# An H3 convolution and ReLU MLP kernel on one core: wider stores and sums of convolution units, row statistics on ScalarE, a new table of moves

## The chip, the cores and the metric

The kernel runs on one core of a Trainium2 chip. The metric is the device time of one execution in microseconds (us). The shown runs of the kernel before took 848.18, 848.7 and 849.46 us; their median is 848.7 us. Below, PE is TensorE, DVE is VectorE, ACT is ScalarE, POOL is GpSimd and SP is SyncE, which issues most of the transfers.

## What is computed

A sequence of 2048 rows of 640 features goes through four layers. Layers 1 and 3 are a gated long convolution, layers 2 and 4 a two-matrix MLP with ReLU. All inputs are float32.

```python
def A(q, k, v, shift_k, ssm_k, ssm_D):        # q is layernorm(x)
    k_shift = sum over t of k shifted by 3 - t, times shift_k[:, 3 - t]
    kv = k_shift * v
    y = irfft(rfft(kv, 2 * S) * rfft(ssm_k, 2 * S))[:S]   # causal, per feature
    return q * (y + kv * ssm_D)
def B(x, w1, w2):                             # x is layernorm(x)
    return maximum(x @ w1, 0) @ w2            # 640 -> 1728 -> 640
x = x + A(layernorm(x), ...); x = x + B(layernorm(x), ...)
x = x + A(layernorm(x), ...); x = x + B(layernorm(x), ...)
```

The convolution's result depends on k, v and the filters alone, so it is computed once and read by both convolution layers.

## The kernel before

**Convolution.** The sequence is cut into 8 chunks of 256 rows, the features into 5 tiles of 128. A unit is one tile of a chunk or two of them: two tiles of one chunk, or one tile of two neighbouring chunks. `transform` makes the spectra of a unit: `at` of kv, `gt` of the filter, 768 numbers per partition and tile (real part, imaginary part, their sum). `spills` (L787 to L791) stores them to DRAM tensors `A` and `G`, one per chunk and tile. `products` multiplies and sums: output chunk a takes the sum over c of A of chunk c times G of chunk a - c. Each product is a DVE `tensor_mul` into a tile `pd` (L847), or straight into the accumulator `pacc` for the first one (L844), and each further one is added by a DVE `tensor_add` of 768 numbers (L848). The spectra of earlier chunks are loaded again at L835. Then come three DVE operations (L878, L880, L881) and one transform back on PE; the result `ys` goes to a DRAM tensor `Y` at L931, one store of 128 x 128 for each tile and each half (row stripe) of a chunk. Tile `ys` lives in a ring `u` of two buffers, which the results `u` of L878 and L880 use too, so a store that has not yet read `ys` holds such a buffer.

**Rows and MLP.** A stripe is 128 rows of a chunk. For the first two chunks each stripe is a step of its own, later both stripes of a chunk go together. `prep` loads `y` from `Y` (L1162), makes the layernorm statistics in `stats`, gates (L1165), adds to the residual `x` (L1172), makes statistics again and cuts the normalized rows into two float16 parts that a transposing DMA brings into `xT` (L1230). In `stats`, DVE forms the negative mean `negm` from the row sums (L1097), ACT the squares (L1100), the root, a Newton step (L1108 to L1112) and the scaled rows (L1122). `main` runs the MLP in seven blocks of hidden features: `mm1` makes `h` in PSUM (L1361 to L1376), ACT writes its high part `hh` (L1516), DVE its low part (L1517; for a single stripe both parts lie in one tile, so this row also reads `hh<-h,hh`), and `mm2` multiplies by w2 one block later (L1345 to L1348). For the last two chunks a form with seven instead of eight block products is used (L1296, L1406). At the end DVE adds to `x` (L1588) with a sum over the row in `sp`; L1596 adds the two parts of that sum into `sums`, which `stats` of the next layer reads.

**Order.** The program records every operation in `Plan` and lays them out with a planner: `order` is a list scheduler that takes, on every engine, the ready operation with the smallest key; `latest` computes from its result the latest time at which each operation may start, and these times are the next keys. `MOVES` is a table: an empty entry means one round of `latest`, another entry (seed, size, from, to, share) shifts the keys of a random share of the operations with a key in that stretch. After the table is worked through, the last order is issued. So an engine executes its instructions in a fixed order, and one that waits holds back all that stands behind it on its engine.

Names in the listings: `hh2_1` is the hidden block 1 of MLP step 2 (steps 0 to 3 are chunk 0: stripe 0 and 1 of the first MLP, stripe 0 and 1 of the second; steps 4 to 7 chunk 1); `pacc2_0`, `pd2_0_4`, `u02_0` belong to the unit that starts at chunk 2, tile 0; `x0_1` is stripe 1 of chunk 0, and `xnA0_1_11`, `negmB0_1_1` belong to its second layer pair (layer 1, stripe 1).

Of the kernel before, what the change touches and what calls it, by code (L numbers as in the profile page):

```python
# [428 lines left out]
def tile_h3_mlp(ctx: ExitStack, tc: tile.TileContext, q, kT, vT, shk, hF, hR, dD, w1, w2, cM, cG, out):  # L429
# [371 lines left out]
    def products(u, at, gt, after):  # L801
# [18 lines left out]
        else:  # L820
            for i, (a, t) in enumerate(u):
                macs += [(i, c, a - c, t) for c in range(a + 1)]
# [926 lines left out]
```

## Time and profile before

| | us |
|---|---|
| median of the shown runs | 848.7 |
| the profiled execution's own time | 848.15 |
| its span in the profile | 846.4 |
| outside the span | 1.75 |

The profile gives for each engine the time in which it was busy. A matmul's record runs until its result has landed, so records overlap, and a short gap between two matmuls does not show as idle time. A row of a group ends with the idle time just before its instructions and what ended it. The mean granted TensorE clock is 0.999 of full speed. Lines with an L are lines of the kernel before; after the change the same statements stand 62 to 88 lines further down (L1517 is then L1605, L848 is L925, L1097 is L1185, L1596 is L1684).

### The profile page before, as it was taken

What the parts mean: (1) busy time and instruction counts of PE and PEld (TensorE: products, weight loads), DVE (VectorE), ACT (ScalarE), POOL (GpSimd) and SP (SyncE); (2) the same over time, 40 slices, a digit from 0 to 9 for tenths busy, and PEclk for the clock granted to TensorE, in tenths of its full rate; (3) what the DMA queues carried; (4) which work ended last, traced back from release to release, by engine and by line L of the source; (5) the groups of instructions that cost most, each with busy time, mean ns of one, the idle gap of its engine ahead of it and who ended that gap; (6) DMA issues with size and microseconds to landing.
All of it is one profiled execution on the core that took longest, in us unless ns stands there. A gap on an engine that the chain in (4) does not pass through costs nothing.

```text
span 846.4 us, 20221 instructions
## 1 busy us (share of the span) xinstructions
PE 835.7 (99%) x7937; PEld 667.4 (79%) x7937; DVE 786.7 (93%) x1514; ACT 510.4 (60%) x1182; POOL 43.8 (5%) x54
## 2 busy tenths in 40 slices
PE   8999999999999999999999999999999999999998
PEld 6987877878878768777787777777777788888886
DVE  7999989999999999999999999999998789989675
ACT  4898587446777565746457474565524487767531
POOL 0000000000001010000100000000000000000000
PEclk9999999999999999999999999999999999999999
DMA  9995868985999999988996977778898466060300
GB/s 312 391 329 193 249 187 233 284 300 167 297 299 248 313 238 279 242 207 234 230 309 180 248 210 207 193 183 220 250 285 271 135 202 142 16 169 13 57 33 33
DMA packets 144914, 181.70 MB, mean 215 GB/s; under 512 B 55089, under 2 KB 98865, under 8 KB 144818
## 3 DMA queue, kind: packets, MB, share of 16 engines
q1 hardware_dynamic: 136498, 169.92, 66.1%
q0 software_dynamic: 8320, 10.49, 7.8%
q8 instruction: 62, 1.02, 0.5%
q14 instruction: 34, 0.28, 0.1%
HBM read 124.59 MB, written 34.08 MB: 187 GB/s over the span
## 4 chain that ended last, share of the span: by engine, by line
PE 76%; DVE 12%; ACT 4%; DMA 3%; issue 2%; SPq 1%; DVEq 0%; ACTq 0%
PE h L1373 8%; PE h L1374 8%; PE h L1376 8%; PE o L1296 7%; PE o L1345 7%; PE o L1346 7%; PE o L1348 6%; PE h L1361 3%; DVE pd L847 2%; DVE pacc L848 2%; PE oc L1345 2%; PE oc L1346 2%; PE oc L1348 2%; PE h L1363 2%; PE h L1406 1%
## 5 line engine op out<-in xcount | busy, mean ns | idle before, releaser
L1373 PE MATMUL h<-xT,w 128*128 128x256 f16 (+1 forms) x1030 | 237.4, 250 | 0.5 <-DVE hh L1531 0.2
L1374 PE MATMUL h<-xT,w 128*128 128x256 f16 (+1 forms) x1030 | 237.3, 250 | 0.0
L1376 PE MATMUL h<-xT,w 128*128 128x256 f16 (+1 forms) x1030 | 237.3, 250 | 0.0
L848 DVE TENSOR_TENSOR pacc<-pacc,pd 128x768 f32<-128x768 f32 x140 | 133.9, 957 | 0.6
L1345 PE MATMUL o<-w,hh 128*128 128x512 f16 x336 | 127.4, 379 | 0.0
L1346 PE MATMUL o<-w,hh 128*128 128x512 f16 x336 | 127.4, 379 | 0.0
L1374 PEld LDWEIGHTS <-w 128*128 128x128 f16 x1130 | 110.6, 98 | 15.8 <-issue 1.5
L1373 PEld LDWEIGHTS <-w 128*128 128x128 f16 x1130 | 110.5, 98 | 14.8
L1376 PEld LDWEIGHTS <-w 128*128 128x128 f16 x1030 | 100.8, 98 | 6.6
L1516 ACT ACTIVATE hh<-h 128x512 f16<-128x512 f32 (+1 forms) x97 | 46.7, 481 | 90.8 <-PE h L1376 64.6
L1345 PEld LDWEIGHTS <-hh 128*128 128x128 f16 x672 | 65.7, 98 | 28.3 <-issue 0.6
L1346 PEld LDWEIGHTS <-hh 128*128 128x128 f16 x672 | 65.8, 98 | 27.1
L847 DVE TENSOR_TENSOR pd<-Ax,Gx 128x768 f32<-128x768 f32 x83 | 78.9, 956 | 2.3 <-DMA Gx<-G 2.3
L1348 PE MATMUL o<-w,hl 128*128 128x512 f16 x208 | 78.9, 379 | 0.0
L1345 PE MATMUL oc<-w,hh 128*128 128x128 f16 x336 | 73.8, 220 | 0.0
L1346 PE MATMUL oc<-w,hh 128*128 128x128 f16 x336 | 73.7, 219 | 0.0
L1348 PEld LDWEIGHTS <-hl 128*128 128x128 f16 x416 | 40.7, 98 | 24.9 <-DVE hl L1517 0.4
L1361 PE MATMUL h<-xT,w 128*128 128x256 f16 (+1 forms) x400 | 57.3, 251 | 0.4 <-DMA xT<-xh 0.4
L589 ACT ACTIVATE tp<-kt,shs 128x256 f32<-128x256 f32 (+1 forms) x78 | 44.4, 576 | 21.2 <-DVE acc L663 14.7
L1348 PE MATMUL oc<-w,hl 128*128 128x128 f16 x208 | 45.6, 219 | 0.2 <-DVE hl L1517 0.2
L847 DVE TENSOR_TENSOR pd<-at,Gx 128x768 f32<-128x768 f32 x46 | 43.5, 957 | 0.0
L1361 PEld LDWEIGHTS <-w 128*128 128x128 f16 x400 | 36.0, 98 | 5.2 <-issue 0.7
(272 smaller groups left out, 1978.7 us busy)
## 6 DMA issues: line engine op xcount, KB each, us to landing
Ax<-A SPq DMA_DIRECT2D x89, 384.0 KB, 4.4
Gx<-G SPq DMA_DIRECT2D x89, 384.0 KB, 4.4
G<-gt SPq DMA_DIRECT2D x30, 384.0 KB, 4.3
A<-at SPq DMA_DIRECT2D x30, 384.0 KB, 6.1
ws<-in_w SPq DMA_DIRECT2D x28, 320.0 KB, 6.5
y<-Y SPq DMA_DIRECT2D x22, 320.0 KB, 3.4
x<-in_q SPq DMA_DIRECT2D x16, 320.0 KB, 5.0
gs<-in_hF SPq DMA_DIRECT2D x20, 256.0 KB, 4.6
```

What stands on the lines that cost most here:

```text
L589: ACT.activation(o[:, i : i + m], kview(i, m, j), AF.Copy, scale=shs[:, t, j : j + 1])
L847: ew(f"mac{j % POOLMOD}", 768, lambda e, pd=pd, av=av, gv=gv: e.tensor_mul(pd.t, av(), gv()), [ax, gx], [pd], pr_)
L848: dve(768, lambda i=i, pd=pd: DVE.tensor_add(acc[:, i], acc[:, i], pd.t), [acc, pd], [acc], pr_)
L1296: PE.matmul(b[:, c : c + w], x, y[:, z : z + w], start=done[i] == 1, stop=end, skip_group_check=fin)
L1345: PE.matmul(z, hh[:, c], wh[:, d], start=(j == JS[0] and i == 0 and (h == 0 or s == S[0])), stop=False)
L1346: PE.matmul(z, hh[:, c], wl[:, d], start=False, stop=end and tail)
L1348: PE.matmul(z, hl[:, c], wh[:, d], start=False, stop=end)
L1361: PE.matmul(p[:, z], wh, xv(t, x), start=b and x == 0, stop=e and x == 1)
L1373: PE.matmul(p[:, z], wh, xv(t, 0), start=b, stop=False)
L1374: PE.matmul(p[:, z], wh, xv(t, 1), start=False, stop=tail and e)
L1376: PE.matmul(p[:, z], wl, xv(t, 0), start=False, stop=e)
L1516: act(2 * R, lambda pv_=pv_, hh=hh: ACT.activation(hh.t, pv_(), AF.Relu), [src], [hh], URGENT)
```

## The change

Four edits and the planner's part in them:

- `spills` stores both tiles of a unit in one transfer: `G<-gt` and `A<-at` are 14 transfers of 128 x 1536 and 2 of 128 x 768 each, where there were 30 of 128 x 768 each. The loads still fetch 768 numbers per partition. The results `ys` of a unit go out in one transfer: 9 of 128 x 4 x 128, 8 of 128 x 2 x 256 and one of 128 x 2 x 128, where there were 70 of 128 x 128.
- In `products` the two tiles of `pd` become the halves of one tile, the products are taken in pairs (both output tiles of a unit for the same c, or neighbouring chunks), and one `tensor_add` adds both halves: 65 of 128 x 1536 and 10 of 128 x 768, where there were 140 of 128 x 768. The multiplications keep their number and size.
- The negative mean (35 instructions of DVE, two small ones of the first MLP stripes stay) and the sum of the two row parts (10 instructions) move from DVE to ACT, 35 and 16 instructions there.
- `Plan` learns to hold a tile whose halves are written by several operations, and `MOVES` has 693 entries instead of 376.

The matmuls are the same in number and shape. SP issues 511 transfers instead of 591, DVE executes 1334 instructions instead of 1444.

The diff, cut to its core:

```diff
 MOVES = ((),) * 4 + (
-    (731577, 15, -65, 335, 10), (84899, 0.5, 663, 1063, 100), ...
+    (309216, 1, -282, 918, 30), (849944, 1, -295, 905, 30), ...
...
+        opens = [t.parent for t in writes if isinstance(t, Sub)]
-        for t in hold:
-            if t.writer is None and t.ring is not None and not t.left and t not in o.new:
+        for t in opens:
+            if t.writer is None and t.ring is not None and t not in o.new:
                 o.new.append(t)
...
     def spills(u, at, gt, pr_):
-        for i, (c, t) in enumerate(u):
-            if c < NC - 2:
-                dma(3072, ... SP.dma_start(G_d[c][t].t, gt[:, i]...), [gt], [G_d[c][t]], max(pr_, SPILL))
-                dma(3072, ... SP.dma_start(A_d[c][t].t, at[:, i]...), [at], [A_d[c][t]], max(pr_, SPILL))
+        n, nm = len(u), "%d_%d" % u[0]
+        for k, x, pat in (("G", gt, "p n a b c -> p n (a b c)"), ("A", at, "p n a b -> p n (a b)")):
+            d = keep(dram, [P, n, 768], k + nm)
+            dma(3072 * n, lambda d=d, x=x, pat=pat: SP.dma_start(d.t, x.t.rearrange(pat)), [x], [d], max(pr_, SPILL))
...
-            pd = T(cv, "pd", 2, [P, 768], f"pd{nm}_{j}")
-            ew(f"mac{j % POOLMOD}", 768, lambda e, ...: e.tensor_mul(pd.t, av(), gv()), [ax, gx], [pd], pr_)
-            dve(768, lambda i=i, pd=pd: DVE.tensor_add(acc[:, i], acc[:, i], pd.t), [acc, pd], [acc], pr_)
+        for j in range(0, len(macs), n):
+            two = macs[j : j + n]
+            if j == 0:
+                dst = [Sub(acc, lambda x, i=i: x[:, i]) for i in range(n)]
+            else:
+                pd = T(cv, "pd", 1, [P, 2, 768], f"pd{nm}_{j}")
+                dst = [Sub(pd, lambda x, i=i: x[:, i]) for i in range(n)]
+            for i, c, m, t in two:
+                (ax, av), (gx, gv) = get("A", c, t), get("G", m, t)
+                ew(f"mac{j % POOLMOD}", 768, lambda e, x=dst[i], ...: e.tensor_mul(x.t, av(), gv()), [ax, gx], [dst[i]], pr_)
...
+            lo, hi = min(x[0] for x in two), max(x[0] for x in two) + 1
+            dve(768 * (hi - lo), ... DVE.tensor_add(acc[:, lo:hi], acc[:, lo:hi], pd[:, lo:hi]), [*sums[lo:hi], *dst[lo:hi]], sums[lo:hi], pr_)
...
-                    dma(512, ... SP.dma_start(Y_d[s][c][:, t * P : t * P + P], ys[:, s, i, :]), [dst[s]], [YW[c_, s, t]], SOON)
+            c, t = u[0]
+            if u[-1][0] == c:
+                f = lambda: SP.dma_start(Y_d[c // 2][:, c % 2, :, t * P : t * P + h].rearrange("s p e -> p s e"), ...)
+            else:
+                f = lambda: SP.dma_start(Y_d[c // 2][:, :, :, t * P : t * P + P].rearrange("s i p e -> p (s i) e"), ...)
+            dma(8 * h, f, dst, [YW[c_, s, t_] for c_, t_ in u for s in range(2)], SOON)
...
-        dve(2, lambda: DVE.tensor_scalar(negm[:, q_], sums[:, q_], -1.0 / D, None, op0=ALU.mult), [sums], [negm], pr)
+        act(2, lambda: ACT.activation(negm[:, q_], sums[:, q_], AF.Copy, scale=-1.0 / D), [sums], [negm], pr, 0.1)
...
-            dve(2, lambda: DVE.tensor_add(sums[:, q_], sp[:, q_, 0], sp[:, q_, 1]), [sp], [sums], URGENT)
+            act(2, lambda: [ACT.activation(sums[:, s : s + 1], sp[:, s, 0:1], AF.Identity, bias=sp[:, s, 1:2]) for s in S], [sp], [sums], URGENT, ...)
```

What the engines' orders show of it at three places. First DVE, in MLP step 2 (chunk 0, stripe 0, second MLP), the rows up to the low part of hidden block 2, before:

```order
L1165 TENSOR_TENSOR xnA0_1_11_1974<-y0_1_11_1261,xnA0_1_11_1974 128x640
L844 TENSOR_TENSOR pacc1_4_1992<-Ax1_4_0_4_1745,gt1_4_1820 128x768
L1172 SCALAR_TENSOR_TENSOR x0_1_308,sums20_1_1_2001<-xnA0_1_11_1974,x0_1_308 128x640
L773 TENSOR_TENSOR at1_4_1915<-at1_4_1915 128x256
L1097 TENSOR_SCALAR negmB0_1_1_2014<-sums20_1_1_2001 128x1
L663 TENSOR_TENSOR acc2_0_1794<-acc2_0_1794,tp12_0_1775 128x512
L1517 SCALAR_TENSOR_TENSOR hh2_2_1982<-h2_2_1939,hh2_2_1982 128x256
```

and the same place now:

```order
L957 TENSOR_TENSOR u01_2_1875<-pacc1_2_1674 128x512
L1605 SCALAR_TENSOR_TENSOR hh2_0_1826<-h2_0_1729,hh2_0_1826 128x256
L959 TENSOR_TENSOR u11_2_1884<-pacc1_2_1674 128x512
L1676 SCALAR_TENSOR_TENSOR x0_1_223,sp0_0_1_1792<-oc1_1021,fac0_1_120,x0_1_223 128x128
L960 TENSOR_TENSOR u11_2_1884<-u11_2_1884,pacc1_2_1674 128x512
L1605 SCALAR_TENSOR_TENSOR hh2_2_1877<-h2_2_1837,hh2_2_1877 128x256
```

The gate and residual of stripe 1 (`xnA0_1_11`, `x0_1` with `sums2`) no longer stand ahead of this row; they come 9 and 11 rows later, and the last sum of the unit at chunk 1, tile 2 has moved ahead.

Second DVE, in MLP step 3 (chunk 0, stripe 1, second MLP), the rows up to the low part of hidden block 4, before:

```order
L1531 SCALAR_TENSOR_TENSOR hh3_6_2630<-hb3_2651,hh3_6_2630 64x128
L848 TENSOR_TENSOR pacc2_0_2595<-pacc2_0_2595,pd2_0_4_2685 128x768
L663 TENSOR_TENSOR acc2_3_2593<-acc2_3_2593,tp12_3_2583 128x512
L1517 SCALAR_TENSOR_TENSOR hh3_4_2752<-h3_4_2710,hh3_4_2752 128x256
L848 TENSOR_TENSOR pacc2_0_2595<-pacc2_0_2595,pd2_0_5_2697 128x768
```

and now:

```order
L959 TENSOR_TENSOR u12_0_2661<-pacc2_0_2208 128x512
L725 TENSOR_TENSOR acc2_3_2457<-acc2_3_2457,tp22_3_2636 128x512
L960 TENSOR_TENSOR u12_0_2661<-u12_0_2661,pacc2_0_2208 128x512
L920 TENSOR_TENSOR pd2_1_2_2705<-Ax2_1_1_1_2520,Gx2_1_1_1_2577 128x768
L920 TENSOR_TENSOR pacc2_1_2722<-Ax2_1_0_2_2249,gt2_1_2596 128x768
L1605 SCALAR_TENSOR_TENSOR hh3_4_2726<-h3_4_2580,hh3_4_2726 128x256
```

The unit at chunk 2, tile 0 is summed up to its end, and the next unit has begun, ahead of a row that before stood in the middle of that unit's sums.

Third ACT, in MLP step 2 around the statistics of stripe 1 of chunk 0, before:

```order
L1516 ACTIVATE hh2_0_1873<-h2_0_1809 128x256
L1100 ACTIVATE jkA0_1_11_1902,ssqA0_1_1_1903<-x0_1_308,negmA0_1_1_1899 128x640
L765 ACTIVATE at1_4_1915<-pr01_4_1896 128x256
L1101 ACTIVATE stdA0_1_1_1925<-ssqA0_1_1_1903,epst_180 128x1
L1516 ACTIVATE hh2_1_1927<-h2_1_1856 128x256
```

and now:

```order
L1604 ACTIVATE hh2_2_1877<-h2_2_1837 128x256
L1684 ACTIVATE sums0_0_1_1896<-sp0_0_1_1792 128x1
L1185 ACTIVATE negmA0_1_1_1904<-sums0_0_1_1896 128x1
L1188 ACTIVATE jkA0_1_11_1907,ssqA0_1_1_1908<-x0_1_223,negmA0_1_1_1904 128x640
L1189 ACTIVATE stdA0_1_1_1928<-ssqA0_1_1_1908,epst_88 128x1
```

The row sum and the negative mean stand on ACT directly ahead of the squares that read them, and the whole chain stands behind hidden block 2 instead of block 0.

More of the change, by code (lines that the diff above doesn't have):

```diff
@@ L211, in op @@
         o.prio, o.cls = (prio, o.seq), prio
-        hold = [t.parent for t in (*reads, *writes) if isinstance(t, Sub)]
+        hold = [t.parent for t in (*writes, *reads) if isinstance(t, Sub)]
+        opens = [t.parent for t in writes if isinstance(t, Sub)]
         reads, writes = ([getattr(t, "tile", t) for t in x] for x in (reads, writes))
         deps, o.new, o.outs = set(), [], []
-        for t in hold:
-            if t.writer is None and t.ring is not None and not t.left and t not in o.new:
+        for t in opens:
+            if t.writer is None and t.ring is not None and t not in o.new:
                 o.new.append(t)
@@ L283, in latest @@
         before = {o: [(d, (0.0 if o.eng == "PE" else PEOUT) if d.eng == "PE" else 0.08 + (o.eng == "PE") * (RPE * LATE(o) + ROOM.get(d.eng, 0.0))) for d in o.deps] for o in out}
-        spare = {}
+        spare, had = {}, {}
         for i, o in enumerate(out):
             for t in o.new:
+                first = t not in had
                 f = spare.setdefault(t.ring, [(-1.0, j, None) for j in range(t.ring.bufs)])
-                f.sort(key=lambda x: x[:2])
-                prev = f.pop(0)[2]
-                for u in users.get(prev, ()):
+                if first:
+                    f.sort(key=lambda x: x[:2])
+                    had[t] = f.pop(0)[2]
+                for u in users.get(had[t], ()):
                     if u is not o and u not in o.deps:
@@ L293, in latest @@
                         left[u] += 1
-                f.append((max(u.ready for u in users[t]), i + len(out), t))
+                if first:
+                    f.append((max(u.ready for u in users[t]), i + len(out), t))
         unit = lambda o: "DMA" if o.nbytes else o.eng
@@ L323, in order @@
                 cand[o.eng].append(o)
-        events, dma, n, out = [0.0], 0.0, 0, []
+        events, dma, n, out, opened = [0.0], 0.0, 0, [], set()
         def fits(o):
@@ L390, in order @@
                 for t in best.new:
+                    if t in opened:
+                        continue
+                    opened.add(t)
                     t.ring.free -= 1
@@ L473, in dtiles @@
         return [[keep(dram, [P, w], f"{nm}{c}_{t}") for t in range(NDT)] for c in range(NC)]
-    A_d, G_d = dtiles("A", 768), dtiles("G", 768)
-    Y_d = [[keep(dram, [P, D], f"Y{s}_{c}") for c in range(NC)] for s in range(2)]
+    kept_u = {}
+    Y_d = [keep(dram, [2, 2, P, D], f"Y{c}") for c in range(0, NC, 2)]
     (URGENT, SOON, SPILL, CONV, LATER, FILL), IDLE = CLS, 9
@@ L819, in products @@
             macs.append((1, b, 0, t))
-        else:
-            for i, (a, t) in enumerate(u):
-                macs += [(i, c, a - c, t) for c in range(a + 1)]
+        elif u[0][0] == u[-1][0]:
+            macs += [(i, c, a - c, t) for c in range(u[0][0] + 1) for i, (a, t) in enumerate(u)]
+        else:
+            raise ValueError(u)
         tl = dict(held)
@@ L833, in get @@
                 x = T(cv, "ag", NAG, [P, 768], f"{k}x{nm}_{c}_{t}")
-                src = (A_d if k == "A" else G_d)[c][t]
-                dma(3072, lambda: SP.dma_start(x.t, src.t), [src], [x], pr_)
+                src, si = kept_u[k, c, t]
+                dma(3072, lambda: SP.dma_start(x.t, src[:, si]), [src], [x], pr_)
                 tl[k, c, t] = (x, lambda: x.t)
             return tl[k, c, t]
-        seen = set()
-        for j, (i, c, m, t) in enumerate(macs):
-            (ax, av), (gx, gv) = get("A", c, t), get("G", m, t)
-            if i not in seen:
-                seen.add(i)
-                dve(768, lambda i=i, av=av, gv=gv: DVE.tensor_mul(acc[:, i], av(), gv()), [ax, gx], [acc], pr_)
+        for j in range(0, len(macs), n):
[7 more added lines that the diff above has]
+                (ax, av), (gx, gv) = get("A", c, t), get("G", m, t)
+                ew(f"mac{j % POOLMOD}", 768, lambda e, x=dst[i], av=av, gv=gv: e.tensor_mul(x.t, av(), gv()), [ax, gx], [dst[i]], pr_)
+            if j == 0:
+                sums = dst
                 continue
-            pd = T(cv, "pd", 2, [P, 768], f"pd{nm}_{j}")
-            ew(f"mac{j % POOLMOD}", 768, lambda e, pd=pd, av=av, gv=gv: e.tensor_mul(pd.t, av(), gv()), [ax, gx], [pd], pr_)
-            dve(768, lambda i=i, pd=pd: DVE.tensor_add(acc[:, i], acc[:, i], pd.t), [acc, pd], [acc], pr_)
+            lo, hi = min(x[0] for x in two), max(x[0] for x in two) + 1
+            dve(768 * (hi - lo), lambda lo=lo, hi=hi, pd=pd: DVE.tensor_add(acc[:, lo:hi], acc[:, lo:hi], pd[:, lo:hi]), [*sums[lo:hi], *dst[lo:hi]], sums[lo:hi], pr_)
+        rd = [acc]
         if not after:
+            rd = sums
             sv = lambda k: acc.r("p c (s b) -> p c s b", s=3)[:, :, k]
@@ L875, in products @@
                 half(1, 1, 1 - ri)
[L876 removed]
+                dve(w, lambda f=f, e=DVE.tensor_add if ri else DVE.tensor_sub: e(f.t, sv(0), sv(1)), rd, [f], pr_)
             elif ri == 0:
[L878 removed]
+                dve(w, lambda f=f: DVE.tensor_sub(f.t, sv(0), sv(1)), rd, [f], pr_)
             else:
[L880 to L881 removed]
+                dve(w, lambda f=f: DVE.tensor_sub(f.t, sv(2), sv(0)), rd, [f], pr_)
+                dve(w, lambda f=f: DVE.tensor_sub(f.t, f.t, sv(1)), [*rd, f], [f], pr_)
             fv = lambda f=f: f.r("p a (b c) -> p a b c", b=2)
@@ L1048, in wcombine @@
                 hi, lo, hv, lv = t, t, (lambda t=t: t[:, 0]), (lambda t=t: t[:, 1])
-            else:
-                hi, lo = (T(*((wp, "w", NW) if j == 4 else (cv, "pd", 2)), [P, 4, H], f"wt{x}{j}", F16, stream=7) for x in "hl")
+            elif j == 4:
+                hi, lo = (T(wp, "w", NW, [P, 4, H], f"wt{x}{j}", F16, stream=7) for x in "hl")
+                hv, lv = (lambda hi=hi: hi.t), (lambda lo=lo: lo.t)
+            else:
+                t = T(cv, "pd", 1, [P, 2, 4, H], f"wt{j}", F16, stream=7)
+                hi, lo = (Sub(t, lambda x, i=i: x[:, i]) for i in range(2))
                 hv, lv = (lambda hi=hi: hi.t), (lambda lo=lo: lo.t)
@@ L1161, in prep @@
                 ys[s] = T(mlp, "y", 2, [P, D], f"y{nm}{s}")
-                dma(4 * cut, lambda s=s: SP.dma_start(ys[s][:, 0:cut], Y_d[s][a].t[:, 0:cut]), [YW[a, s, t] for t in range(NDT) if (a, s, t) in YW and t * P < cut], [ys[s]], SOON)
+                dma(4 * cut, lambda s=s: SP.dma_start(ys[s][:, 0:cut], Y_d[a // 2][s, a % 2, :, 0:cut]), [YW[a, s, t] for t in range(NDT) if (a, s, t) in YW and t * P < cut], [ys[s]], SOON)
             xns = stats(xs, sums, "A" + nm, S)
@@ L1595, in main @@
             sums = small("sums", f"sums{nm}")
-            dve(2, lambda: DVE.tensor_add(sums[:, q_], sp[:, q_, 0], sp[:, q_, 1]), [sp], [sums], URGENT)
+            act(2, lambda: [ACT.activation(sums[:, s : s + 1], sp[:, s, 0:1], AF.Identity, bias=sp[:, s, 1:2]) for s in S], [sp], [sums], URGENT, 0.1 + 0.2 * (len(S) - 1))
             SUMS[a, S] = sums
```

30 lines of the change are left out of this document (18 added, 12 removed), and 179 rows, old and new, of the table MOVES.

## The prediction

> **What bounds the kernel now.** I read the page first, then busy time by stretch, then the waits by engine, then the timeline at the longest wait inside the program. The page gives the span, the busy time of each engine, and the shares of the chain that ended last:
>
> ```profile
> span 846.4 us, 20221 instructions
> ...
> PE 835.7 (99%) x7937; PEld 667.4 (79%) x7937; DVE 786.7 (93%) x1514; ACT 510.4 (60%) x1182; POOL 43.8 (5%) x54
> ...
> PE 76%; DVE 12%; ACT 4%; DMA 3%; issue 2%; SPq 1%; DVEq 0%; ACTq 0%
> ```
>
> PE is idle for 846.4 - 835.7 = 10.7 us. The change leaves the matmuls as they are, so these are nearly all that it could win. The stretches show where they lie (start and end, length, then busy us and count of PE, PEld, DVE, ACT, POOL, then clock, DMA share, GB/s):
>
> ```profile
> 0.00:20.00 20.00, 16.20 (x89) 13.79 (x90) 14.03 (x32) 9.17 (x19) 1.79 (x14) 1.00 0.91 307
> ...
> 100.00:150.00 50.00, 48.70 (x554) 39.16 (x552) 46.05 (x96) 37.32 (x101) 0.00 (x0) 1.00 0.75 225
> 150.00:200.00 50.00, 50.00 (x585) 41.23 (x584) 49.55 (x90) 23.39 (x55) 0.00 (x0) 1.00 0.84 273
> 200.00:250.00 50.00, 49.40 (x590) 39.70 (x589) 48.77 (x96) 34.84 (x86) 1.88 (x2) 1.00 0.89 257
> ...
> 450.00:500.00 50.00, 49.79 (x409) 37.02 (x408) 49.94 (x79) 30.81 (x73) 5.07 (x5) 1.00 0.84 228
> ...
> 700.00:750.00 50.00, 49.61 (x447) 41.54 (x446) 44.75 (x118) 37.08 (x85) 0.00 (x0) 1.00 0.41 97
> 820.00:847.00 27.00, 22.23 (x250) 18.61 (x248) 15.10 (x38) 6.00 (x13) 0.00 (x0) 0.97 0.07 26
> ```
>
> The start leaves 3.8 us, the end 4.77 us (0.6 of which is past the span); both hang on first loads and a last chain which the change leaves alike. Between them stand 1.30 + 0.60 + 0.21 + 0.39 = 2.5 us, and some 0.2 in stretches not shown. DVE is as full as PE from 150 to 500 (49.94 of 50). So two engines are full, and the waits say which waits for which:
>
> ```profile
> PE oc L1348 <- DVE hh L1517: 1.2, 2, 0.9
> ...
> PE h L1361 <- DMA xT<-xh: 0.4, 1, 0.4
> PE hb L1529 <- ACT tb L1520: 0.3, 1, 0.3
> PE oc L1348 <- DVE hl L1517: 0.2, 1, 0.2
> PE h L1373 <- DVE hh L1531: 0.2, 1, 0.2
> ```
>
> Columns are total us, times, longest. Inside the program PE waits for DVE's L1517, once for a transfer, once for ACT. The longest case is at 110 us (start, length, instruction, idle before it):
>
> ```profile
> 109.98 0.22 PE L1345 MATMUL oc<-w,hh 128*128 128x128 f16 x1
> 110.04 0.22 PE L1346 MATMUL oc<-w,hh 128*128 128x128 f16 x1
> 111.16 0.23 PE L1348 MATMUL oc<-w,hh 128*128 128x128 f16 x1 [0.91 <-DVE hh L1517]
> 111.23 0.38 PE L1345 MATMUL o<-w,hh 128*128 128x512 f16 x1
> ```
>
> ```profile
> 104.12 0.69 DVE L880 TENSOR_TENSOR u<-pacc 128x512 f32<-128x512 f32 x1 [1.11 <-DMA Y<-ys]
> ...
> 107.33 0.82 DVE L1165 TENSOR_TENSOR xnA<-y,xnA 128x640 f32<-128x640 f32 x1
> 108.08 0.95 DVE L844 TENSOR_TENSOR pacc<-Ax,gt 128x768 f32<-128x768 f32 x1
> 108.94 0.82 DVE L1172 SCALAR_TENSOR_TENSOR x<-xnA,x 128x640 f32<-128x640 f32 x1
> ...
> 109.69 0.42 DVE L773 TENSOR_TENSOR at<-at 128x256 f32<-128x256 f32 x1
> 110.03 0.14 DVE L1097 TENSOR_SCALAR negmB<-sums 128x1 f32<-128x1 f32 x1
> 110.09 0.68 DVE L663 TENSOR_TENSOR acc<-acc,tp 128x512 f32<-128x512 f32 x1
> 110.69 0.42 DVE L1517 SCALAR_TENSOR_TENSOR hh<-h,hh 128x256 f16<-128x256 f32 x1
> ```
>
> The row that PE needs stands behind six others. PE's starts are 1.12 us apart (110.04 to 111.16) where the next ones are 0.07 apart (111.16 to 111.23), so the stall costs 1.05 us, of which 0.91 shows. A kernel in which both engines are full gains where an instruction stands earlier, and little where work merely gets less.
>
> **The change, part by part.** *Sums in one operation.* The rows for this, for the small operations taken from DVE and for their like on ACT:
>
> ```profile
> L848 DVE TENSOR_TENSOR pacc<-pacc,pd 128x768 f32<-128x768 f32 x140 | 133.9, 957 | 0.6
> ...
> L663 DVE TENSOR_TENSOR acc<-acc,tp 128x512 f32<-128x512 f32 x51 | 35.2, 690 | 0.0
> L1097 DVE TENSOR_SCALAR negmB<-sums 128x2 f32<-128x2 f32 x13 | 2.2, 167 | 0.0
> L1596 DVE TENSOR_TENSOR sums<-sp 128x2 f32<-128x2 f32 x6 | 1.0, 163 | 0.0
> ```
>
> ```profile
> L1101 ACT ACTIVATE stdB<-ssqB,epst 128x2 f32<-128x2 f32 x13 | 3.8, 291 | 0.3
> L1112 ACT ACTIVATE nmrB<-rstdB,negmB 128x1 f32<-128x1 f32 x30 | 7.2, 281 | 0.1
> ```
>
> From 512 to 768 numbers an operation grows by 957 - 690 = 267 ns, so 1.04 ns a number: an add of 1536 lasts 957 + 800 = 1757 ns as an estimate. But records of DVE overlap: the product at 108.08 lasts 0.95, and the next starts at 108.94, after 0.86. Two adds therefore hold DVE 1.72 us, and one wide one 0.86 + 0.80 = 1.66: 0.06 saved, 65 times 4 us. The bounds are nothing, if a wide add behind its own second product waits out its full record (0.95 - 0.86 = 0.1 lost), and 65 x (2 x 957 - 1757) = 10.2, were records not to overlap. I take 4.
>
> [...]
>
> *Small operations.* 45 leave DVE. One there holds it 0.06 (110.03 to 110.09 above): 2.7 us less on DVE. On ACT, 51 come at 281 to 291 ns of record, at most 51 x 0.29 = 15 us, on an engine that is busy for 510 of 846 us. With the sums DVE has 7 us less to do. What hides this is PE: where PE is never idle, DVE's saving turns into DVE's waiting. ACT waited for the negative mean behind DVE's queue:
>
> ```profile
> ACT jkB L1100 <- DVE negmB L1097: 10.2, 11, 2.4
> ACT jkA L1100 <- DVE negmA L1097: 9.9, 10, 2.6
> ```
>
> These 20 us go, and the statistics of a stripe come up to 2.6 us earlier. Only the 0.39 in which PE waits for `xT` could use that. Were that cover gone (ACT late with `hh`), one or two operations of 0.29 stand ahead of it. I charge 0 for the move, with bounds of -0.4 and +0.6.
>
> *Stores.* 30 fewer for the spectra and 52 fewer for `Y`:
>
> ```profile
> A<-at SPq DMA_DIRECT2D x30, 384.0 KB, 6.1
> G<-gt SPq DMA_DIRECT2D x30, 384.0 KB, 4.3
> ...
> Y<-ys SPq DMA_DIRECT2D x70, 64.0 KB, 3.4
> ```
>
> SP's queue is shorter by 80 of 591 issues. A double spill carries twice the bytes; bounded by two landing in turn it lands 6.1 us later, 4.3 for `G`. Its reader is a unit of a later chunk, tens of us away, and no wait of PE above leads to such a load. `Y` in one store can start only when both halves stand (they are made two operations of 0.42 us apart), and one landing replaces up to eight. Bounds: -0.3 to +0.5 (a `u` buffer held longer; DVE waits for one 1.11 us at 104.12). I take 0.
>
> *Order.* This is where the money lies. At the first place of the order shown above, `xnA0_1_11` and `x0_1` (1.6 us) no longer stand ahead of hidden block 2's low part, nor does the first product of a unit. Adding up starts for all DVE rows ahead of `hh2_2` and all PE rows ahead of its reader, DVE comes 4.3 us earlier relative to PE than before. So the stall at 110 us goes: **-1.05**. Of the 0.60 between 200 and 250 the largest piece is the second wait of that row, 1.2 - 0.9 = 0.3; by the same count its low part stands 5.1 us better after, the next block's 0.6 worse, and I take only the one: **-0.3**. From 300 us on that lead is larger by up to 5 us, from 575 on by 5 to 8, and `hl` at 482 us stands 3.7 us better: **-0.5** of the 0.21 + 0.39.
>
> At the second place it goes the other way. The low part of `hh3_4` and its reader stand so before:
>
> ```profile
> 149.19 0.42 DVE L1517 SCALAR_TENSOR_TENSOR hh<-h,hh 128x256 f16<-128x256 f32 x1
> ```
>
> ```profile
> 150.04 0.22 PE L1348 MATMUL oc<-w,hh 128*128 128x128 f16 x1
> ```
>
> It is ready at 149.61, 0.43 us ahead of its reader's start; the signal takes 0.05 (110.69 + 0.42 = 111.11 against 111.16 at the stall), so 0.4 is slack. After the change 140.5 us of DVE work stand ahead of it instead of 134.6, and 144.6 us of PE work instead of 141.2: added up as before, 5.9 us more against 3.4. The lead shrinks by 2.5, and PE would wait 2.5 - 0.4 = 2.1 us, if DVE worked as before. But DVE was idle for 50 - 46.05 = 3.95 us between 100 and 150, waiting for ACT or a store, and with earlier units ahead it can use that. Bounds 0 to +2.1; I take the nearer one with some loss: **+0.6**.
>
> Sum: -1.05 - 0.3 - 0.5 + 0.6 = **-1.25 us**. Against the profiled execution's 848.15 that is 846.9; it stood 0.55 below the median of 848.7, so the forecast is 847.45, said as **847.5**.
>
> **The rivals.** *DVE is the bound (R1).* PE's 99% is made of overlapping records: a matmul of 0.22 us starts every 0.06. If PE runs a little behind DVE all along from 150 to 700, as DVE's 49.94 of 50 suggests, DVE's 7 us less pass into the time, up to the gaps and what the records hide. With 0.15 hidden in each of some ten gaps (1.05 - 0.91 at the long one) that is 2.7 + 1.5 = 4.2, so 848.7 - 4.2 = **844.5**. Against it: the starts above follow each other at 0.06 (109.98 to 110.04), as short as I found them anywhere for this form.
>
> [...]
>
> *DVE falls behind at 125 to 185 us (R2).* The price worked out above, 2.1 us, is paid once, because PE and DVE stay full until 500 and nothing gives it back; the stall at 110 us is lost again too, since PE then reaches `hh3_4` that much earlier. It decides as soon as DVE's waits in 100 to 150 stay above 3.95 - 2.1 = 1.85 us. That gives 848.7 + 2.1 = **850.8**. For it: DVE's waits there are for ACT's `hh` and a store, and ACT gets more to do there. Against it: DVE has fewer small rows in the same place.
>
> *Waits are only exchanged (R3).* The new table of moves places all 1334 DVE rows anew, and as many gaps of 0.2 to 0.9 us arise as went: 848.0 to 849.5, **848.7**. For it: after the change PE still depends on one row of L1517 per block. The change would then do what it says, and nothing for the time.
>
> **How the numbers follow.** A difference of 0.2%, 1.7 us, is about what a measurement of this kernel can tell from none; the bounds are 847.0 and 850.4. Forecast 0.52, from 846.4 (DVE covers the 0.6, the statistics give 0.4) to 848.6 (neither of the two small gains comes, and the stores cost 0.3); below 847.0 lies 0.19, within 0.33. R1 0.17, faster. R2 0.20: slower 0.16, within 0.04 where part of the price is covered. R3 0.11: 0.10 within, 0.01 slower. So faster 0.36, same 0.47, slower 0.17. The range from 844.8 to 851.0 leaves out the better half of R1 and the worse half of R2, some 0.18.
>
> **What would show it.** For the sum: the 128x1536 add at about 1757 ns, DVE's small L1097 and L1596 gone, DVE busy at 786.7 - 10.2 - 45 x 0.165 = 769 us in records; no wait of PE for L1517's successor near 110 us; PE idle in 100 to 150 below 0.7; ACT's waits for the negative mean gone. R1 would show PE idle for 8 us, at the start and the end alone, and the gain spread from 150 to 700. R2 would show PE idle of 1 us or more between 125 and 185 released by `hh`. R3 would show small waits at new places. The forecast is wrong if the start or the end changes by over 1 us, which I took as alike, or if ACT becomes late with `hh` by its 51 new operations.

## The result and the profile after

The changed kernel takes 847.06 us (median of 22 runs, 844.87 to 850.39) against 849.04 for the kernel before in as many. The ratio is 0.9974, with a 95% interval of 0.9963 to 0.9985: 2.2 us less, by the interval 1.3 to 3.1. The forecast was 847.5 against 848.7, a ratio of 0.9986. Way and range were right, but the largest part of the gain that the experiments find lies in a part that I had priced at nothing, and the largest term of my sum brought nothing by itself. That the number came near is luck.

The page of the execution that was profiled:

```profile
span 848.6 us, 20004 instructions
...
PE 836.8 (99%) x7937; PEld 668.0 (79%) x7937; DVE 778.7 (92%) x1404; ACT 518.3 (61%) x1233; POOL 43.8 (5%) x54
...
PE 70%; DVE 19%; DMA 4%; ACT 3%; issue 2%; SPq 1%; DVEq 0%; POOLq 0%; ACTq 0%
```

DVE is busy for 8 us less and ACT for 8 more, as the edits would have it, but the span, 848.6, is longer than the 846.4 shown of before, for a kernel that is faster by its medians. This execution took 850.39 us, the longest of its 22. Two of its rows stand out:

```profile
0.00:20.00 20.00, 16.02 (x79) 13.40 (x80) 12.83 (x29) 10.34 (x23) 1.81 (x14) 0.91 0.87 290
```

```profile
PE h L1449 <- DMA xT<-xh: 2.2, 1, 2.2
```

The granted clock was 0.91 in the first 20 us (1.00 before), and PE waited once, near 266 us, 2.2 us for the transposing transfer of `xT`. The 22 executions of the changed kernel lie up to 5.5 us apart, those of the kernel before 5.7, so a profile of one says where a kernel can lose, and the medians say how much. The changed kernel was therefore run and profiled again (`after_again` below, 848.47 us). Its stretches, to be held against the rows of before:

```profile
100.00:150.00 50.00, 50.00 (x570) 40.23 (x568) 49.44 (x95) 38.91 (x106) 0.00 (x0) 1.00 0.77 235
150.00:200.00 50.00, 50.00 (x595) 41.64 (x593) 48.47 (x82) 26.01 (x63) 0.00 (x0) 1.00 0.82 268
200.00:250.00 50.00, 49.62 (x597) 39.85 (x595) 48.09 (x89) 37.34 (x96) 1.88 (x2) 1.00 0.92 278
250.00:300.00 50.00, 48.88 (x444) 37.63 (x443) 46.38 (x67) 28.98 (x68) 6.27 (x6) 1.00 0.96 270
300.00:350.00 50.00, 49.55 (x409) 37.86 (x408) 49.94 (x79) 32.85 (x78) 6.29 (x6) 1.00 0.95 263
450.00:500.00 50.00, 50.00 (x417) 37.89 (x416) 49.82 (x72) 29.22 (x70) 4.16 (x4) 1.00 0.82 220
700.00:750.00 50.00, 50.00 (x452) 42.15 (x450) 43.82 (x114) 38.79 (x92) 0.00 (x0) 1.00 0.38 95
750.00:800.00 50.00, 49.60 (x501) 41.86 (x499) 40.99 (x113) 31.72 (x76) 0.00 (x0) 1.00 0.30 67
```

Between 100 and 150 us PE's idle 1.30 us is gone, and DVE, idle for 3.95 us there before, is idle for 0.56. The gaps of 450 to 500 and 700 to 750 are gone as well. New ones stand in 250 to 300 (1.12), 300 to 350 (0.45) and 750 to 800 (0.40). PE's waits name them:

```profile
PE oc L1433 <- ACT hh L1604: 0.7, 1, 0.7
PE h L1461 <- DVE hl L1610: 0.5, 1, 0.5
PE oc L1436 <- DVE hl L1605: 0.4, 1, 0.4
...
PE o L1384 <- DVE gs L1600: 0.4, 1, 0.4
```

The visible idle time of 20 to 820 us is thus 2.4 us after and 2.7 before. The two profiles show exchanged waits; they do not show the 2 us.

### The profile page after: what moved, and what is told of

Its sections match the earlier page's. It is cut to its first block, busy times and chain, and to the rows that moved or that the text cites. A ratio compares the mean times of both kernels' runs of the same rounds, so it can differ in the third digit from the quotient of the medians.

```text
span 848.6 us, 20004 instructions
## 1 busy us (share of the span) xinstructions
PE 836.8 (99%) x7937; PEld 668.0 (79%) x7937; DVE 778.7 (92%) x1404; ACT 518.3 (61%) x1233; POOL 43.8 (5%) x54
## 4 chain that ended last, share of the span: by engine, by line
PE 70%; DVE 19%; DMA 4%; ACT 3%; issue 2%; SPq 1%; DVEq 0%; POOLq 0%; ACTq 0%
PE h L1461 8%; PE h L1462 8%; PE h L1464 8%; PE o L1434 6%; PE o L1433 6%; PE o L1384 6%; PE o L1436 6%; PE h L1449 3%; DVE pd L920 3%; DVE pacc L925 3%; PE oc L1433 2%; PE oc L1434 2%; PE pg L754 2%; PE h L1451 1%; PE oc L1436 1%
## 5 line engine op out<-in xcount | busy, mean ns | idle before, releaser
L925 DVE TENSOR_TENSOR pacc<-pacc,pd 128x1536 f32<-128x1536 f32 (+1 forms) x75 | 123.3, 1643 | 0.5
```

The source lines that it names most:

```text
L925: dve(768 * (hi - lo), lambda lo=lo, hi=hi, pd=pd: DVE.tensor_add(acc[:, lo:hi], acc[:, lo:hi], pd[:, lo:hi]), [*sums[lo:hi], *dst[lo:hi]] ...
```

## The experiments

All were timed beside the kernel before. Wherever the text says "after's order", PE's rows are the same one for one, and on the other engines only the rows of the edit differ. Where it says "undone", the instructions change and stand where the planner had put the operation.

**The changed kernel again, and three edits undone in its order.** The first three edits:

```diff
 # split_adds
-DVE.tensor_add(acc[:, lo:hi], acc[:, lo:hi], pd[:, lo:hi])
+[DVE.tensor_add(acc[:, i], acc[:, i], pd[:, i]) for i in range(lo, hi)]
 # stats_dve
-ACT.activation(negm[:, q_], sums[:, q_], AF.Copy, scale=-1.0 / D)
+DVE.tensor_scalar(negm[:, q_], sums[:, q_], -1.0 / D, None, op0=ALU.mult)
-[ACT.activation(sums[:, s : s + 1], sp[:, s, 0:1], AF.Identity, bias=sp[:, s, 1:2]) for s in S]
+DVE.tensor_add(sums[:, q_], sp[:, q_, 0], sp[:, q_, 1])
 # order_only: both, and the stores of split_stores below
```

> The changed kernel, unaltered, as the standard for the three others. Both theories: ratio to before 0.9974, about 846.8 us. Theory O (the order: DVE's rows that PE waits for stand earlier, the stall at 110 us is gone) expects in its profile no PE idle between 100 and 150 us. In the profile shown, PE waited 2.2 us for xT (a transfer) near 250 us and the clock was 0.91 in the first 20 us; if these belong to single executions, this profile is free of them and its span is 844 to 846 us.

Measured: 848.51 us median, ratio 0.9981 (0.9963 to 1.0000). As theory O has it, PE shows no idle time between 100 and 150 us. The low clock and the long wait for `xT` are absent, so they belong to single executions, but the span of 846.7 us is longer than the 844 to 846 expected without them.

> After's order on every engine; each of the 65 wide sums is issued as two adds of 768 in its place. DVE gets 65 x 0.06 = 4 us more to do. Theory O (order alone, PE is the bound, DVE's saving is hidden): as the changed kernel, within 0.5 us. Theory D (DVE is the bound from 150 to 600 us and its saving passes into the time): 3 to 4 us above the changed kernel, so above the kernel before.

Measured: 850.49, ratio 1.0008 (0.9991 to 1.0024), 2.0 us above `after_again` on the same chip.

> After's order on every engine; the 35 negative means and 10 row sums are issued on DVE, at the same points of the program, instead of on ACT. Theory O: within 0.5 us of the changed kernel. Theory D: 45 x 0.06 = 2.7 us above it. Theory S (statistics: ACT's 20 us of waits behind DVE's queue held up the rows that PE needs): 1 to 3 us above it, with PE waiting for xT.

Measured: 855.73, ratio 1.0066 (1.0042 to 1.0089), 7.2 us above `after_again`.

> After's order with all three edits undone: sums as two adds of 768, statistics on DVE, spectra and results stored in pieces of one tile (82 more transfers). Theory O: ratio to before 0.997 to 0.998, as the changed kernel. Theory D: 6 to 7 us above the changed kernel, ratio to before about 1.005. A value between (2 to 4 us above) would say that order and edits share the gain.

Measured: 859.15, ratio 1.0100 (1.0067 to 1.0134), 10.6 us above `after_again`.

Theory O, my own, falls with the last: after's order with before's instructions is slower than the kernel before by about 8.5 us (1.0%). The sizes fit none of the theories: the statistics cost more than any of them said, and all three edits together more than the 6 to 7 us of theory D. Nor is the saving of 7 us of DVE's time the cause by its size, since the statistics, 2.7 us of DVE, cost 7.2 us, and the sums, 4 us of DVE, cost 2.0. What the statistics do is seen in ACT's waits, in `stats_dve` first and then in `after_again`:

```profile
ACT jkB L1188 <- DVE negmB L1185: 32.8, 16, 8.2
...
ACT jkA L1188 <- DVE negmA L1185: 14.7, 11, 3.0
```

```profile
ACT negmB L1185 <- DVE x L1260: 16.3, 9, 6.6
...
ACT sums L1684 <- DVE x L1676: 8.2, 5, 4.1
...
ACT sums L1684 <- DVE x L1542: 2.9, 1, 2.9
```

With the negative mean on DVE, ACT stands 47.5 us in front of the squares, up to 8.2 at a time: until `x` is there, and then until DVE has worked through what is queued ahead of a 0.17 us operation. The longest case in `stats_dve` shows both parts, DVE first and then ACT:

```profile
556.08 0.09 DVE L1260 DVE_READ_ACCUMULATOR x<-xnA,x 128x1 f32 x1
556.08 0.96 DVE L920 TENSOR_TENSOR pd<-Ax,Gx 128x768 f32<-128x768 f32 x1
556.95 0.17 DVE L1185 TENSOR_SCALAR negmB<-sums 128x2 f32<-128x2 f32 x1
```

```profile
557.15 0.83 ACT L1188 ACTIVATE jkB<-x,negmB 128x640 f32<-128x640 f32 x1 [8.23 <-DVE negmB L1185]
...
557.98 0.57 ACT L1604 ACTIVATE hh<-h 128x512 f16<-128x512 f32 x1
```

`x` and its row sum stand at 556.17 and the squares start at 557.15. So 7.25 us of this wait are for `x`, and 0.98 for the product that is queued ahead of the negative mean and for the mean itself; the high part `hh` of a hidden block stands right behind. With the mean on ACT, ACT waits for `x` alone, 27.4 us, 20 less in the same order, and what stands behind the squares can start earlier. For PE the difference shows as idle time: 8.9 us between 20 and 820 us in `stats_dve` against 2.4 in `after_again`. Its waits in `stats_dve` are mostly for rows of ACT and DVE; those for `xT`, which theory S had named, are 0.8 us:

```profile
PE pt L801 <- ACT ob L781: 1.5, 2, 0.9
PE hb L1461 <- DVE hl L1605: 1.4, 1, 1.4
...
PE oc L1433 <- ACT hh L1604: 1.1, 1, 1.1
PE oc L1436 <- DVE hh L1605: 1.1, 2, 0.6
PE h L1449 <- DMA xT<-xh: 0.8, 3, 0.4
```

PE in `order_only`, stretch 100 to 150:

```profile
100.00:150.00 50.00, 48.70 (x556) 38.97 (x554) 48.53 (x100) 37.27 (x100) 0.00 (x0) 1.00 0.81 232
```

and its waits in the part that I had counted on:

```profile
120.33 0.22 PE L1461 MATMUL h<-xT,w 128*128 128x128 f16 x1 [0.38 <-DVE hh L1619]
129.86 0.23 PE L1449 MATMUL h<-xT,w 128*128 128x128 f16 x1 [0.88 <-DMA xT<-xh]
```

The stall at 110 us is away, as the order said it would be, and as much idle time as before, 1.30 us in the stretch, stands at 120 and 130 us. With before's instructions this order only moves it; with the edits the stretch is full (50.00 above).

**One row, and one part, in before's order.** The lines that only pick a row are given in words, here and in a later edit.

```diff
 # before_hh2_early, behind the planner, on the finished order
+low = the DVE operation on hh2_2 and h2_2
+ahead = the first DVE operation on pacc1_4
+out.remove(low)
+out.insert(out.index(ahead), low)
 # before_stats_act
-DVE.tensor_scalar(negm[:, q_], sums[:, q_], -1.0 / D, None, op0=ALU.mult)
+ACT.activation(negm[:, q_], sums[:, q_], AF.Copy, scale=-1.0 / D)
-DVE.tensor_add(sums[:, q_], sp[:, q_, 0], sp[:, q_, 1])
+[ACT.activation(sums[:, s : s + 1], sp[:, s, 0:1], AF.Identity, bias=sp[:, s, 1:2]) for s in S]
```

> The kernel before with one row of DVE moved: the low part of hh2_2 stands ahead of the first product of the unit at chunk 1, tile 4, five rows earlier. Nothing else differs. Theory O (a stall of 1.05 us at 110 us, as the prediction's largest term): PE's wait of 0.91 us there goes, ratio 0.9988 (1.05 us less). Rival: the time comes back at a later row, as DVE and PE are both full to 500 us: no stall at 110, ratio 1.000, and another wait for hh or hl between 115 and 250 us is longer by about as much.

Measured: 849.32, ratio 1.0004 (0.9995 to 1.0013). The rival holds. DVE and PE in its profile (its lines stand four further down), first the two low parts, then the wait of PE that follows:

```profile
109.22 0.42 DVE L1521 SCALAR_TENSOR_TENSOR hh<-h,hh 128x256 f16<-128x256 f32 x1
...
115.83 0.42 DVE L1521 SCALAR_TENSOR_TENSOR hh<-h,hh 128x256 f16<-128x256 f32 x1
```

```profile
116.30 0.22 PE L1377 MATMUL hb<-xT,w 128*128 128x128 f16 x1 [1.12 <-DVE hh L1521]
```

The row for block 2 is early and PE no longer waits for it; PE then waits 1.12 us for the next block's at 116 us. DVE shows no wait between 108 us and that row, so it was late as a whole, not one of its rows. ACT was late too. In the same profile it waits for the negative mean and writes the high part that this row reads only behind the statistics:

```profile
111.68 0.83 ACT L1104 ACTIVATE jkB<-x,negmB 128x640 f32<-128x640 f32 x1 [2.69 <-DVE negmB L1101]
...
115.16 0.36 ACT L1520 ACTIVATE hh<-h 128x256 f16<-128x256 f32 x1
```

The high part is ready at 115.52 and DVE takes it at 115.83. With ACT's rows as they ran, no order of DVE's rows behind that mean could have brought this row more than 0.3 us earlier.

The same profile has PE busy for 50.00 of 50 in the two stretches in which the profile of before lost 0.21 and 0.39:

```profile
450.00:500.00 50.00, 50.00 (x413) 37.34 (x412) 49.93 (x80) 30.81 (x72) 5.07 (x5) 1.00 0.88 231
...
700.00:750.00 50.00, 50.00 (x452) 41.96 (x450) 45.45 (x119) 38.25 (x87) 0.00 (x0) 1.00 0.40 96
```

The order there is that of before. As far as a second execution can show, those gaps belonged to the first, and there was nothing for the change to mend.

> The kernel before, its order kept on every engine, with the 35 negative means and 10 row sums issued on ACT at the same points of the program. Theory S (the statistics' way through DVE's queue holds up ACT, and with it the hidden blocks; moving them is worth something by itself): 1 to 4 us less than before. Theory F (each order is fitted to the operations it was made for; what stats_dve lost is the loss of the fit): the same as before or slower, since ACT now waits in its queue for the row sums of DVE.

Measured: 847.62, ratio 0.9982 (0.9971 to 0.9992): 1.5 us less than before, with no new order, no wider sum and no merged store. ACT's wait in front of the squares, 20.1 us in before, becomes this wait in front of the negative mean:

```profile
ACT negmB L1097 <- DVE x L1172: 7.5, 6, 2.1
```

With 0.5 us in front of the row sums that is 8.0. Theory S holds: the statistics are worth something by themselves, and the forecast of theory F (no gain, or a loss) did not come. The 1.5 us rest on the times. The one profile (846.96 us) bears them out in part: PE is idle for 1.8 us between 20 and 820 us against 2.7 in before, but 0.57 of these 0.9 lie in the two stretches just named, in which `before_hh2_early` lost nothing either. Taking the statistics away from the order made for them cost 7.2 us, giving them to an order not made for them brought 1.5. The fit of an order to its operations would explain the difference, but no run shows it alone.

**The stores.** Each store of a unit is issued in pieces of one tile, which makes 28 more transfers for the spectra (14 units of two tiles, two tensors) and 52 for the results, 80 in all (the 30 and the 82 of the expectations are a miscount):

```diff
-SP.dma_start(d.t, x.t.rearrange(pat))
+[SP.dma_start(d[:, i], x.t.rearrange(pat)[:, i]) for i in range(n)]
-SP.dma_start(Y_d[c // 2][:, c % 2, :, t * P : t * P + h].rearrange("s p e -> p s e"), ...)
+[SP.dma_start(Y_d[c_ // 2][s, c_ % 2, :, t_ * P : t_ * P + P], ys[:, s, i, :]) for i, (c_, t_) in enumerate(u) for s in range(2)]
```

> After's order; only the stores of the spectra and of the results are issued in pieces of one tile (30 and 52 more transfers). The prediction's term of 0 says: as the changed kernel, within 0.5 us. From order_only against split_adds and stats_dve (10.6 - 2.0 - 7.2) some 1.4 us more are left for the stores, if the three losses add up.

Measured: 847.83, ratio 0.9988 (0.9978 to 0.9999). Against the changed kernel's 0.9974 and 0.9981 that is 0.6 to 1.2 us more. Its interval overlaps both of theirs, so it is not told apart from nothing, nor from the 1.4 us that the other losses leave.

**DVE freed.**

```diff
-DVE.tensor_add(acc[:, lo:hi], acc[:, lo:hi], pd[:, lo:hi])
+DVE.tensor_add(acc[:, lo:hi, 0:384], acc[:, lo:hi, 0:384], pd[:, lo:hi, 0:384])
```

> After's order; every sum of products adds only the first half of each 768 columns, so DVE has 65 x 0.8 = 52 us less to do; the result lacks that part of the sums. If PE is the bound and only its gaps are to be had (PE idle between 20 and 820 us of after_again: 2.4 us, and 0.15 hidden in each of some eight): at most 3.6 us less than the changed kernel, ratio to before 0.993 to 0.995. If DVE is the bound from 150 to 600 us beneath PE's overlapping records: 5 us or more less, ratio below 0.992.

Measured: 847.17, ratio 0.9978 (0.9965 to 0.9991). DVE in the part in which it had been full:

```profile
300.00:350.00 50.00, 50.00 (x415) 38.25 (x414) 44.65 (x75) 34.90 (x87) 6.29 (x6) 1.00 0.86 250
```

DVE has five of 50 us to spare here, and some 50 less to do in all, and the time is the changed kernel's; the ratio lies above both forecasts. In the changed kernel DVE is not the bound beneath PE. More DVE work costs (2.0 us in `split_adds`), less brings nothing, so DVE has just enough room there. Rival R1 spoke of the kernel before, which was not freed in this way. There one of its own stretches speaks against R1, since PE was busy throughout while DVE stood idle for 2 us:

```profile
400.00:450.00 50.00, 50.00 (x420) 39.22 (x418) 47.95 (x72) 24.74 (x52) 7.49 (x7) 1.00 0.92 249
```

**A stall of the changed kernel.** ACT, DVE and PE in `after_again` at 275 us:

```profile
274.72 0.63 ACT L672 ACTIVATE hr<-hr 128x512 f32<-128x512 f32 x1 [4.80 <-DMA gs<-hr]
275.25 0.58 ACT L1604 ACTIVATE hh<-h 128x512 f16<-128x512 f32 x1
```

```profile
275.87 0.69 DVE L1605 SCALAR_TENSOR_TENSOR hl<-h,hh 128x512 f16<-128x512 f32 x1 [2.34 <-ACT hh L1604]
```

```profile
275.89 0.23 PE L1433 MATMUL oc<-w,hh 128*128 128x128 f16 x1 [0.68 <-ACT hh L1604]
```

ACT waits 4.8 us for an adding transfer of POOL, and the high part that PE needs stands behind. The edit exchanges the two:

```diff
+i, j = out.index(turn), out.index(high)       # turn: hr4_1 on ACT, high: hh8_0 on ACT
+late = the operations of out[i:j] on hr4_1
+out = [o for o in out[: j + 1] if o not in late] + late + out[j + 1 :]
```

> After's order with two rows of ACT exchanged: the high part of hh8_0 stands ahead of the sign change of hr4_1, which waits 4.8 us for a transfer of POOL. In the profile of after_again PE loses 0.84 + 0.60 us there (275 us), and DVE is idle for 2.3 us. Theory G (a stall mended pays where the engines behind it have room, as DVE has here, and does not where DVE is full, as at 110 us): 1.4 us less than the changed kernel, ratio to before 0.996. Rival (each stall mended comes back at the next row, as in before_hh2_early): no less than the changed kernel, with PE's waits between 276 and 310 us longer by about 1.4 us.

Measured: 847.40, ratio 0.9984 (0.9969 to 0.9999). No gain over the changed kernel shows in the times. Its profiled execution (845.54 us; lines stand five further down) has the stall away:

```profile
250.00:300.00 50.00, 49.78 (x455) 38.89 (x454) 48.00 (x70) 29.22 (x66) 6.27 (x6) 1.00 0.99 276
```

but that is no proof of the edit, since the transfer itself was early in this execution:

```profile
272.45 0.63 ACT L677 ACTIVATE hr<-hr 128x512 f32<-128x512 f32 x1 [0.73 <-DMA gs<-hr]
```

ACT could go on at 272.45 instead of 274.72, 2.3 us earlier, so hardly anything would have been late in the old order either. Theory G and its rival are not told apart.

**The price of the small operations on ACT.**

```diff
-ACT.activation(negm[:, q_], sums[:, q_], AF.Copy, scale=-1.0 / D)
+[ACT.activation(negm[:, q_], sums[:, q_], AF.Copy, scale=-1.0 / D) for _ in range(2)]
-... for s in S]
+... for s in S for _ in range(2)]
```

> After's order; each of the 51 small operations that moved to ACT is issued twice. ACT has 51 x 0.2 = 10 us more to do, and each chain of statistics is longer by 0.2 to 0.3 us. The prediction's term (0, as ACT is busy for 61%) says: within 0.5 us of the changed kernel. If the place of these operations in ACT's queue costs what they last, whenever a hidden block's high part stands behind them: 2 us or more above it.

Measured: 852.06, ratio 1.0033 (1.0020 to 1.0046), 0.0052 to 0.0059 above the changed kernel's two ratios, which is 4.4 to 5.0 us. ACT is idle for 39% of the span in `after_again` (busy for 517.8 of 846.7 us), and some 40% of what the 51 copies last (35 of 0.20 us and 16 of 0.287, 11.6 us) comes through all the same. The largest of PE's waits in it:

```profile
PE h L1449 <- DMA xT<-xh: 2.3, 2, 2.0
```

The copies lengthen the chain of statistics by 0.2 to 0.3 us each, and the chain ends in the transposed rows that PE reads. That this wait comes from them is not shown, since the changed kernel's first profile had it too.

**Without the table.**

```diff
-MOVES = ((),) * 4 + (...)
+MOVES = ((),) * 4
```

> The changed code with the table of moves cut to its first four empty entries, so the planner's plain order. To be read against before_no_table. Theory S (the edits, the statistics above all, are worth something in any order): 2 us or more less than before_no_table. Theory F (the gain lies in the table that was made for these operations): within 1 us of before_no_table, or above it. Both: 5 to 25 us above the kernel before, ratio 1.006 to 1.03.

Measured: 849.21, ratio 1.0011 (0.9989 to 1.0033).

> The code of before with the table of moves cut to its first four empty entries. Ratio to before 1.006 to 1.03; the table is then worth 5 to 25 us to the kernel before. For the theories see after_no_table.

Measured: 854.53, ratio 1.0071 (1.0055 to 1.0088).

Without the table the changed code is 854.53 - 849.21 = 5.3 us faster, as theory S had it. That both would be at 1.006 or above did not come: the changed code's 1.0011 is not told apart from the kernel before. The two plain orders differ, since the planner makes each from other operations, so the 5.3 us hold the edits and their order together. PE's longest wait inside the program is for `xT`, in `before_no_table` and then in `after_no_table`:

```profile
PE h L1297 <- DMA xT<-xh: 4.4, 2, 2.4
```

```profile
PE h L1332 <- DMA xT<-xh: 2.0, 3, 1.0
```

That this is part of the 5.3 us is not shown: the two profiled executions took 852.95 and 853.33 us, so the second is the slower one, 4 us above its median. ACT's wait for the statistics does not explain them either: it rose from 29.9 us (in front of the squares) to 35.8 (in front of the row sums and the negative mean).

The table was worth about 6 us to the kernel before (1.0071 to 1) and about 2.5 to 3 to the changed one (1.0011 to 0.9974 or 0.9981). Both tables end near 847 to 849.

## Why the prediction came out right, and where its steps were wrong

**What bounds.** PE bounds, and the gain is bounded by its gaps: right, shown for the changed kernel by `short_adds`. DVE was busy for 729.3 us there instead of 778.6, and the time, 847.17 us, stayed the changed kernel's, so the starts 0.06 apart, which I had held against R1, were a good witness here. "DVE is as full as PE from 150 to 500" was read too broadly: it is busy for 48.77 of 50 us in 200 to 250 and for 47.95 in 400 to 450.

**Order, the failed step.** "This is where the money lies" is wrong. The sum had -1.05 for the stall at 110 us, -0.3 for 200 to 250 and -0.5 for two later gaps, and all its -1.25 came from rows that stand earlier or later. Of these, the 0.3 nearly came in the profile (PE idle for 0.38 us there instead of 0.60). Put earlier alone, the row gave nothing (1.0004), as PE waited 1.12 us at the next block. The two later gaps were absent from a second execution in the same order. And after's order with before's instructions, for which it was not made, costs 8.5 us. I read a stall as the fault of the rows ahead of the late one, where at the next row DVE, without a wait since 108 us, and ACT, which had stood 2.69 us for the negative mean, were late as well.

**Statistics, the term that was mis-sized.** "I charge 0 for the move, with bounds of -0.4 and +0.6": `before_stats_act` measures -1.5 (-2.5 to -0.7), most of the whole change. I had the row for it, 20 us of ACT's waiting for the negative mean, and counted only the chain that ends in `xT`. I left out that ACT stands still in the meantime, with hidden blocks behind it. That ACT is busy for only 510 of 846 us is no cover for an operation on the chain: `stats_twice` costs 4.4 to 5.0 us. "These 20 us go" was half right: the waits for the negative mean went, and in after's order 27.4 us of waiting for `x` stand in their place.

**Sums.** The price of the instruction was right:

```profile
L925 DVE TENSOR_TENSOR pacc<-pacc,pd 128x1536 f32<-128x1536 f32 x65 | 114.2, 1757 | 0.5
```

```profile
260.73 1.75 DVE L925 TENSOR_TENSOR pacc<-pacc,pd 128x1536 f32<-128x1536 f32 x1
262.39 0.69 DVE L822 TENSOR_TENSOR sl<-pt,sh 128x512 fp32r<-128x512 f32 x1
```

1757 ns as estimated, and 1.66 us from start to start. That nothing of it passes into the time was wrong by 2.0 us in after's order, where half of DVE's 4 us counts; in before's order no run shows it. The sign "DVE busy at 769 us in records" did not come, as DVE is busy for 778.6. I took 157 ns off for each sum, but the busy time counts an overlap of two records once: in `split_adds` 140 adds of 958 ns are busy for 128.3 us, not 134.1, and DVE as a whole has 781.7, only 3.1 us more, which is near the 4 of the estimate. Nor does the time move by the 10.2 us that the records alone would give (2 x 957 - 1757 = 157 ns for each of 65).

**Stores.** 0, and 0.6 to 1.2 not told from 0. Two counts were wrong: the spectra have 28 transfers fewer, not 30, which with 52 makes the 80 of SP, and one landing replaces at most four stores of `Y` (70 became 18), not eight.

**Thinner lead at 125 to 185 us.** I took +0.6 and R2 had 2.1. Neither came: PE is busy for 50.00 of 50 in both stretches, and DVE's idle 3.95 us became 0.56. The cover that I named was there.

**New gaps.** R3's exchange of waits did happen, 1.12, 0.45 and 0.40 us in three stretches that had no gap before, and I had put nothing into the sum for it. The forecast had a part within its bound of 0.2% and a part beyond it. The measured middle, 0.26% less, lies beyond, with an interval of 0.15 to 0.37% that reaches into the other part.

**What stays open.** The stretches of the two kernels' profiles add up to nearly the same lost time, and the medians differ by 0.7 to 2.0 us. In which stage a typical execution of before loses more than the profiled one (848.15 against a median of 849.04) no profile here shows. Nor is it settled how much of 7.2 us is the fit of the order and how much the statistics: in like orders ACT's wait falls (47.5 to 27.4, 20.1 to 7.5), but from before to after it does not (20.1 to 27.4), nor between the two plain orders (29.9 to 35.8). So the length of ACT's wait by itself does not give the time. That another order lets ACT wait where it costs less is argued only. What the sums and the order bring beyond the statistics' 1.5 of 2.2 us lies within the intervals.

## What to carry to other kernels

In this kernel a tiny operation was better placed on the engine that waits for it: what counted was the queue ahead of it and who stood still meanwhile, not its 0.17 or 0.20 us. A stall names the last late row; before pricing its removal, look whether the engine behind it is late for the next row as well. An edit was worth 7.2 us in one order and 1.5 in another, so an edit is best tried in more than one order, the planner's plain one among them.

## What the runs showed of the hardware

Sums of 512, 768 and 1536 numbers lie on one line: 690 and 957 ns in the kernel before and 1757 in `after_again`, 1.04 ns for each further number. In the rows shown DVE starts the next operation 0.08 to 0.09 us before such a record ends (110.09 + 0.68 against 110.69, 260.73 + 1.75 against 262.39). An ACT operation on one or two numbers takes 197 to 203 ns as a scaled copy (L1185) and, on one number, 287 when it adds a second operand (L1684), against 167 and 163 on two numbers on DVE in the kernel before (L1097, L1596). Executions of the changed kernel lie 5.5 us apart (844.87 to 850.39). Two things differ between profiled ones: a granted clock of 0.91 in the first 20 us (the first profile) or 1.00 (`after_again`), and transfers that land some us later, as the one for which ACT waited until 274.72 us in `after_again` and until 272.45 in `after_hh8_early`.
